# Band masks by edge, loads by half, and a new order of steps in a two-stage attention kernel

## The chip, the cores and the metric

The kernel runs on one core of a Trainium2 chip. A core has a matrix engine (PE, with its weight loads, PEld), a vector engine (DVE), a scalar engine (ACT), a general engine (POOL) and an engine that only issues transfers (SP). They run their own instruction streams, each in order, and wait for one another by semaphores. SP, ACT and POOL each issue DMA transfers into a queue of their own. The metric is the device time of one execution in microseconds. 181.07 us is the median of three runs of the kernel before.

## The reference

Two layers. The first is a local attention over 4 batches, 8 heads, 768 positions and a head size of 64. Each query sees the keys less than 16 positions away, and one summary for each of the 24 blocks of 32 positions: the maximum of the block's keys, and the mean of its values.

```python
k_sum = k.reshape(B, H, nb, block, D).max(axis=3)
v_sum = v.reshape(B, H, nb, block, D).mean(axis=3)
mask_l = np.abs(pos[:, None] - pos[None, :]) < window
scores_s = scale * np.einsum('bhsd,bhnd->bhsn', q, k_sum) + np.log(block)
scores_all = np.concatenate([np.where(mask_l, scores_l, -1e9), scores_s], axis=-1)
attn = softmax(scores_all) @ np.concatenate([v, v_sum], axis=2)
```

The second takes the result, with the heads joined (512 columns), through four causal attention experts of one head each; a gate picks two of the four per position and weighs their outputs.

```python
for e in range(E):
    q, k, v = x @ wq[e], x @ wk[e], x @ wv[e]
    ye = causal_softmax(scale * q @ k.T) @ v @ wo[e]
    out += (gate weight of e, 0 if not among the top two) * ye
```

## The kernel before

**Names of steps.** The kernel is a list of some 740 steps. Each step is a few instructions, with a kind, a batch b, and a pair of heads c (0 to 3) or a group g of two pairs; `sc010` is the first half of the scores of batch 0, pair 1. `TABLE` gives the order in which the steps are issued, the engine of each (V, A, G, S, P for DVE, ACT, POOL, SP, PE) and the buffers that it takes. Since each engine runs in order, the order of an engine's steps in the table is its queue. Step numbers in the table count the steps as they are declared. An entry `f` puts in matmuls on zeros; the first number is the bank, the second their count.

**First layer, for each pair of heads.** `dk`, `dq` load four heads of keys or queries, cast to half precision, from POOL; for batch 0, group 0 in two parts of two heads each (`parts`). Both parts write one buffer `kn` or `qn`, and whoever reads it waits for both. `dv` loads the values of a pair in 24 blocks of 64 positions, rows 0 to 63 of a block, beginning 16 positions before it (L277 to L281). `hc` copies rows 0 to 31 of each next block into rows 64 to 95, so that a block holds its whole band of 96 positions; it leaves out the last block of each head. `vq` copies the last rows of a head and zeroes rows 0 to 15 of each head's first block (L288). `vz` once zeroes the rows behind each head's end, and `vone` writes the column that sums the weights, zero where the value rows are zeroed. The block sums of the values come in two ways: `bs` (matmuls with a selection matrix, L306), `be` (their sum out of PSUM, DVE, L324) and `ds` (a copy into rows 96 to 119 of every block); or, for the groups in `TREE`, `dvs` (a second load of the values from SP, L341), `tr` (a tree of additions on POOL, L355) and `ds`. Then `tk` turns the keys (L373), `kw` lays them out by blocks, `rk` takes the maxima (L393), `ksc` appends them; `tq` and `cq` turn the queries. `sc` starts with a matmul that writes the band mask (L426) and adds the scores of six blocks (L432); `ex` is the exponential (L440), `av` the product with the values (L450), `rc` and `xm` the division, `tx` a transpose (L477), `hi` and `lo` a split into two half-precision numbers.

**Second layer, for each batch.** `pp` (projections, L640) and `pc`; `vp` (values and gate, L570), `lg`, `v2`; `ga` to `gc` the gate; `sp` (scores, L664), `es` (exponential, L672), `dm` (causal cut on POOL, L677), `aw` (L688), `r2`, `wv`, `tw`, `ct`, `op` (L750), `oc`, and `od` (the store).

The buffers are few: three of `kn` and `qn`, six of values, one tree buffer, eight PSUM banks. The copies are recorded under the lines of a helper: L164 on ACT, L166 on the others. The first layer of one batch is interleaved with the second layer of the one before.

Of the kernel before, what the change touches and what calls it, by code (L numbers as in the profile page):

```python
# [25 lines left out]
TREE = {(1, 1), (2, 0), (2, 1), (3, 0), (3, 1)}  # L26
# [26 lines left out]
4,V, 18,S,0 10,G, 8,V, 17,V, 0,V, f,P,0.8 7,V, 112,S, 20,A, 13,G,0 15,G, 14,G,0 16,G, 30,G,1 11,G, 1,G, 61,P,1  # L53
5,V, 62,A,0 63,V,0 44,P,0 64,V, 45,A,1 f,P,2.5 31,G,1 78,P,0 79,A,2 9,G, 2,G, 3,V, 46,V,0 65,P,2 48,P,3 99,P,0
204,G,0 49,V,0 82,P,1 66,A,1 24,S,1 19,V, 205,G,2 47,A, 32,S,2 21,P,3 80,V,0 22,V,0 6,G, 52,P,4 83,A,2 81,A,
50,P,1 53,A,0 95,P,6 100,A,0 246,P,7 51,A,1 96,V,1 97,V,0 26,V, 98,G, 229,P,3 67,P,4 68,A,2 25,G, 224,S,0 69,P,0
250,P,2 251,V,1 84,P,4 70,A,3 230,A,0 23,G, 216,G,0 86,P,0 33,G, 27,P,6 28,V,1 87,A,4 247,A,2 85,A,5 248,V,0
34,A, 55,P,0 231,V,1 54,P, 29,G, 56,V,0 103,P,4 104,A,1 35,P,6 71,P,4 57,V,0 36,V,1 38,S,3 39,G, 58,P,0 59,V,0
37,A, 120,G, 60,V,0 72,P, 73,V,0 74,V,0 89,P,6 88,P, 40,A, 101,P,0 102,A,5 41,P,4 280,P,5 90,V,0 91,V,1 42,V,1
43,V, 232,A, 281,A,1 249,G, 254,P,0 255,A,4 252,P,6 92,P,2 93,A,1 206,S,4 209,S,0 233,P,4 234,V,1 116,S,0 115,S,  # L60
117,S,1 225,G, 94,V,1 263,P,5 113,S, 105,P,0 211,A, 106,P, 253,A,5 107,V,0 108,V,1 235,P,2 236,A,1 114,A, 75,P,6
109,P,0 110,V,2 111,V,2 76,A,3 210,G, 208,G, 207,G, 77,V,3 221,S,2 212,P,2 213,V,1 122,G, 264,A,2 166,P,3
168,P,0 217,G,2 119,A, 167,A,0 226,G,0 218,S,3 12,G, 121,A, 169,V,1 227,G, 127,P,6 129,V,0 179,P,0 180,A,0
282,V,1 128,V,0 265,V,0 182,P,2 183,A, 130,P,4 132,A, 124,P,0 214,G, 125,A, 385,S,0 283,V, 131,V, 126,A, 176,P,2
170,P,6 171,A, 267,P,4 139,P,0 133,V,5.0 134,A, 177,A, 223,V, 268,V,0 140,V,2 228,G, 237,P,6 284,P,4 238,A,3
215,G, 266,G, 285,V,1 269,P,2 173,P,0 270,A,2 172,G, 240,P,6 135,V, 136,V,0 239,P, 174,A, 271,P,2 272,A,1 118,S,
123,A, 185,P,0 137,P,4 286,P,2 186,A, 287,A,3 241,V,0 242,V,1 243,P,6 288,P,0 138,V,0 150,P,4 222,V, 289,A,0
257,P,2 244,V,0 245,V,0 151,A,1 220,G, 144,P,0 378,G,2 256,P, 258,V,0 259,V,1 377,G,0 424,P,4 425,V,1 145,A,
386,G, 403,P,5 404,A,1 379,A,0 290,P,0 291,P, 156,P,4 157,A, 147,P,2 260,P,6 261,A,1 390,G,1 219,G, 181,G,
274,P,4 273,P, 148,A, 184,G, 292,V,0 293,V,0 262,V,1 153,P,0 154,A, 275,V,0 276,V,1 187,G, 565,G,1 294,P,2  # L70
295,A,2 632,P,6 296,V,2 387,G,0 392,S,1 437,P,7 277,P,4 278,A,3 149,G, 146,G, 155,G, 279,V,3 420,P,0 407,P,1
559,S,0 566,S,3 421,V,2 438,A,0 408,A,0 339,P,2 340,A,1 341,P,4 178,G, 388,G, 391,G,2 158,G, 175,G, 141,P,2
633,A,2 190,P,0 188,P, 342,A,0 189,P, 346,P,4 422,V,0 423,G, 352,P,6 564,G,0 389,V,2 405,V,0 380,G, 142,A,
191,V,0 192,V,0 406,V, 300,P,2 347,A,0 143,G, 303,P,4 382,A, 301,A,0 302,V,1 381,G, 152,G, 193,P,0 353,A, 305,A,
355,P,6 394,V, 304,A, 560,G, 349,P,2 356,A, 357,G, 297,P,4 350,A, 561,G,0 310,P,6 299,V, 159,P,2 298,A, 439,V,0
194,V,0 348,G, 384,G, 161,P, 160,P, 162,V,0 358,P,0 311,A,2 359,A, 411,P,6 412,A,2 343,P,4 344,A, 312,P,0
# [12 lines left out]
635,A,4 486,P,0 487,A,1 602,P,2 603,A,2 525,G, 337,P,4 338,V,0 611,P,7 612,V,2 534,G, 558,G, 636,P,0 637,A,3
520,P,4 481,A, 482,V, 521,A, 522,G, 519,G, 484,P,2 529,P,0 613,V,1 485,A,0 530,A, 615,P,7 616,V,2 483,V,0  # L90
587,P,4 588,P, 589,V,0 614,G, 600,P,2 601,A,0 575,G, 488,P,0 489,A,1 567,G, 490,G, 374,P,6 375,A,1 590,V,1
571,G, 531,G, 368,P,4 369,V,0 619,P,0 620,A,5 617,P,2 618,A,1 591,P,6 500,P,4 592,V,0 622,P,0 621,P, 593,V,0
370,A, 623,V,0 624,V,1 605,P,2 604,P, 606,V,0 503,P,6 501,A, 504,A, 607,V,0 625,P,0 626,A,1 627,V,1 494,P,4
639,P,6 528,G, 491,P,2 638,P, 495,A, 497,P,0 505,G, 492,A, 608,P,4 498,A, 640,V,0 371,P,2 641,V,1 642,P,0 502,G,
609,V,2 535,P,6 643,A,3 610,V,2 537,P, 644,V,3 536,P, 538,V,0 372,A,0 658,P,4 660,P,0 693,P,2 659,V,0 539,V,0
661,A,1 373,A, 493,G, 677,P,0 678,A,0 665,P,6 666,A, 694,V,2 674,P,4 651,P,0 668,P,6 671,P,2 675,A, 669,A,
670,G, 200,S, 691,P,4 672,A, 652,V,0 653,V,1 662,P,6 540,P,0 663,A, 692,A,0 648,P,2 649,V, 496,G, 650,V, 499,G,
507,P,6 541,V,0 506,P, 508,P, 509,V,0 510,V,0 376,S, 707,P,2 701,P,0 708,A,1 645,P,4 511,P,6 698,P,2 702,A,
647,V, 646,V, 673,G, 667,G, 699,A, 512,V,2 710,P,0 711,A, 695,P,4 676,G, 709,G, 696,A, 703,G, 545,P,6 664,G,
679,G, 654,V,2.0 655,A, 681,P,0 656,V, 682,P, 546,A,0 547,S, 704,P,3 705,A, 657,V,0 680,P, 683,V,0 684,V,0  # L100
687,V, 548,P,6 549,A,1 550,S, 542,P,2 688,V, 543,A,2 544,S, 700,G, 697,G, 706,G, 712,G, 715,P,4 714,P, 713,P,
720,V,0 689,P,2 690,A,0 685,P,0 721,V,1 722,P,6 686,A, 723,V,2 716,V, 717,V, 733,P,6 736,A,0 737,A, 718,P,4
730,P,7 719,V, 724,P,4 734,V,1 735,S, 731,V,2 732,S, 725,A,0 726,S, 727,P,0 728,A,1 729,A,
# [51 lines left out]
def make_plan(nc, T, q, k, v, moe_w_gate, moe_wq, moe_wk, moe_wv, moe_wo, out):  # L155
# [3 lines left out]
    def en(e):  # L159
        return getattr(nc, ENG[e])  # L160
# [17 lines left out]
    vones, vz, kwpad, v2one, knpad = st("vones"), st("vz"), st("kwpad"), st("v2one"), st("knpad")  # L178
# [7 lines left out]
    def masks(e):  # L186
        nc.gpsimd.memset(T["mt"], 0.0)
        for h0 in (0, 64):
            w = T["mt"][h0:h0 + 64, 0:WIN]
            nc.gpsimd.affine_select(w, w, [[-1, WIN]], AL.is_ge, NEG, base=31, channel_multiplier=1)  # L190
            nc.gpsimd.affine_select(w, w, [[1, WIN]], AL.is_ge, NEG, base=-1, channel_multiplier=-1)
# [8 lines left out]
    def vone(e):  # L200
        t = T["vball"]
        en(e).memset(t[0:96, :, 0:24, 64:65], 1.0 / XS)
        en(e).memset(t[96:128, :, 0:24, 64:65], 32.0 / XS)
        en(e).memset(t[0:16, :, 0:24:NQ, 64:65], 0.0)
        en(e).memset(t[64:96, :, NQ - 1:24:NQ, 64:65], 0.0)
        en(e).memset(t[64:80, :, NQ - 1:24:NQ, 64:65], 1.0 / XS)
# [8 lines left out]

    def vzero(e):
        t = T["vball"]
        en(e).memset(t[64:96, :, NQ - 1:24:NQ, 0:64], 0.0)
# [17 lines left out]
    def vtzero(e):  # L236
        for t in T["vt"]:
            en(e).memset(t, 0.0)

    qn, kn = {}, {}  # L240
# [694 lines left out]
```

## Time and profile before

| | |
|---|---|
| runs | 180.6, 181.07, 185.0 us |
| profiled execution | 177.54 us, its span 175.8 us |
| mean granted clock of PE | 0.956 |
| busy: PE, PEld | 148.6, 108.8 us |
| busy: DVE, ACT, POOL | 122.7, 124.9, 104.9 us |
| moved by DMA | 25.60 MB |
| chain that ended last | PE 42%, DMA 24%, ACT 10%, POOL 8%, DVE 7%, issue 6% |

A busy share is a mean over the whole span, and matmuls are pipelined, so PE's busy time is no measure of its peak. Where the time goes is read stage by stage, from the idle time of PE and what ended it. The chain names, for each moment, what the work that ended last was waiting for.

### The profile page before, as it was taken

To read this page: it belongs to the slowest core of one execution; us is meant where nothing else is said; L and a number is where in the kernel's file an instruction comes from. 1 tells how busy PE (TensorE), PEld (TensorE's weight loads), DVE (VectorE), ACT (ScalarE), POOL (GpSimd) and SP (SyncE) were. 2 spreads that over 40 slices of the span, in tenths; PEclk is the share of its full clock that TensorE was granted. 3 is DMA by queue.
4 is the path that set the end of the run, shared out by engine and by line. 5 is a ranking of instruction groups with operands and counts; after the bars stand their busy time and mean duration, and the time that the engine had idled before them with its cause. 6 is when DMAs were issued, how large, how long until landed. Compare 5 with 4: busy or idle time off the path is not lost.

```text
span 175.8 us, 6926 instructions
## 1 busy us (share of the span) xinstructions
PE 148.6 (85%) x3005; PEld 108.8 (62%) x3005; DVE 122.7 (70%) x244; ACT 124.9 (71%) x160; POOL 104.9 (60%) x181
## 2 busy tenths in 40 slices
PE   0667973999896999999998899869999999999760
PEld 0236752798764777867755488648765875675420
DVE  6345566579795987799985788872896986277630
ACT  2344686169948986899687977868989583969650
POOL 8962059746965798379959999927978200324100
PEclk9995699579999999999999999999999999999998
DMA  5999999999998699999969938991001502101846
GB/s 94 181 195 198 216 186 148 152 201 193 153 197 228 80 170 188 173 194 171 150 106 175 181 55 191 250 248 49 4 4 62 183 4 75 44 4 35 300 157 229
DMA packets 44894, 25.60 MB, mean 146 GB/s; under 512 B 33344, under 2 KB 39744, under 8 KB 44864
## 3 DMA queue, kind: packets, MB, share of 16 engines
q1 hardware_dynamic: 33200, 16.08, 47.7%
q0 software_dynamic: 6432, 6.29, 23.5%
q10 hardware_dynamic: 5232, 2.79, 7.7%
q8 instruction: 23, 0.38, 1.0%
q14 instruction: 7, 0.06, 0.1%
HBM read 25.16 MB, written 6.29 MB: 179 GB/s over the span
## 4 chain that ended last, share of the span: by engine, by line
PE 42%; DMA 24%; ACT 10%; POOL 8%; DVE 7%; issue 6%; POOLq 0%; ACTq 0%; DVEq 0%
DMA vb<-in_v_dram 11%; PE ps L450 9%; DMA kn<-in_k_dram 8%; PE ps L640 6%; DMA qn<-in_q_dram 5%; PE ps L570 4%; PE ps L688 4%; ACT a L672 3%; PE ps L664 3%; PE ps L750 3%; PE ps L477 3%; PE ps L373 3%; POOL vb L166 3%; PE ps L306 2%; PE ps L426 2%
## 5 line engine op out<-in xcount | busy, mean ns | idle before, releaser
L672 ACT ACTIVATE a<-ps 128x1024 f16<-128x1024 f32 (+1 forms) x48 | 42.5, 922 | 5.6 <-PE ps L664 4.0
L677 POOL TENSOR_SCALAR_AFFINE_SELECT a<-a 128x256 f16<-128x256 f16 x48 | 19.1, 421 | 28.4 <-ACT a L672 25.1
L440 ACT ACTIVATE aT<-ps 120x768 f32<-120x768 f32 x32 | 25.4, 815 | 9.1 <-PE ps L432 6.9
L450 PE MATMUL ps<-vb,aT 120*64 120x65 f32 x768 | 28.1, 231 | 3.3 <-issue 2.3
L450 PEld LDWEIGHTS ps<-vb,aT 120*64 120x64 f32 x768 | 25.6, 145 | 6.4 <-issue 4.0
L355 POOL TENSOR_TENSOR vt<-vt 120x1024 f32<-120x1024 f32 (+3 forms) x20 | 24.1, 1205 | 1.0
L640 PE MATMUL ps<-hi,wqk 128*128 128x384 f16 x128 | 22.6, 326 | 0.4 <-DVE lo L495 0.3
L166 POOL COPY vb<-vb 16x128 f32<-16x128 f32 (+1 forms) x20 | 14.1, 712 | 9.7 <-DMA vb<-in_v_dram 8.9
L164 ACT COPY kw<-ps 128x1152 f16<-128x1152 f16 x13 | 14.4, 1122 | 7.5 <-PE ps L373 7.5
L393 DVE TENSOR_REDUCE ks<-kw 128x24 f16<-128x768 f16 x16 | 14.9, 943 | 4.8 <-ACT kw L164 4.5
L640 PEld LDWEIGHTS <-wqk 128*128 128x128 f16 x128 | 11.9, 97 | 8.4 <-issue 1.2
L664 PE MATMUL ps<-qk,qk 64*128 64x512 f16 (+3 forms) x128 | 15.8, 307 | 1.0 <-DVE wT L166 0.7
L570 PE MATMUL ps<-wvg,hi 128*128 128x264 f16 x96 | 13.9, 275 | 3.0 <-ACT a L672 1.5
L465 DVE TENSOR_TENSOR x<-ps,rec 128x768 f32<-128x768 f32 x16 | 15.3, 958 | 1.0 <-PE ps L477 0.5
L495 DVE TENSOR_TENSOR lo<-ps,hi 128x768 f16<-128x768 f32 x16 | 15.0, 955 | 1.5 <-ACT hi L164 1.0
L166 POOL COPY vb<-vu 24x768 f32<-24x768 f32 x18 | 14.8, 823 | 1.0
L688 PE MATMUL ps<-v,a 128*128 128x65 f16 x336 | 12.3, 194 | 0.6 <-POOL a L677 0.6
L688 PEld LDWEIGHTS <-a 128*128 128x128 f16 x336 | 11.2, 97 | 2.3 <-issue 0.9
L750 PE MATMUL ps<-wo,wT 128*128 128x512 f16 x48 | 12.0, 380 | 0.5 <-DVE wT L166 0.5
L432 PEld LDWEIGHTS <-kw 64*128 64x128 f16 x384 | 10.4, 98 | 2.8 <-issue 0.7
L426 PE MATMUL ps<-pi,mt 64*128 64x384 f16 x64 | 11.4, 345 | 0.3 <-DVE qT L166 0.3
L432 PE MATMUL ps<-qT,kw 64*128 64x64 f16 x384 | 11.5, 195 | 0.0
(106 smaller groups left out, 269.7 us busy)
## 6 DMA issues: line engine op xcount, KB each, us to landing
vb<-in_v_dram SPq DMA_DIRECT2D x12, 400.0 KB
out_dram<-ob SPq DMA_DIRECT2D x8, 512.0 KB
vt<-in_v_dram SPq DMA_DIRECT2D x20, 192.0 KB
kn<-in_k_dram POOLq DMA_DIRECT2D x7, 384.0 KB, 7.6
qn<-in_q_dram POOLq DMA_DIRECT2D x7, 384.0 KB, 6.3
out_dram<-ob ACTq DMA_DIRECT2D x3, 512.0 KB
vb<-in_v_dram ACTq DMA_DIRECT2D x2, 400.0 KB
vb<-in_v_dram SPq DMA_DIRECT2D x2, 384.0 KB
```

The source lines that it names most:

```text
L166: en(e).tensor_copy(dst, src)
L355: en(e).tensor_tensor(y, p, q_, AL.add)
L432: nc.tensor.matmul(s[:, hp, 64 * t:64 * t + 64], T["kw"][kw.slot][r, tt, :], T["qT"][qT.slot][r].rearrange("c (s p) -> c s p", s=8)[:, :, ...
L440: nc.scalar.activation(T["aT"][aT.slot][0:KR], pbank(sc, 2)[0:KR, :, 0:384], AF.Exp, scale=SCALE)
L450: nc.tensor.matmul(pbank(av, 2)[o:o + 64, u, 65 * (2 * (t // 2) + hp):65 * (2 * (t // 2) + hp) + 65], a[0:KR, hp, 64 * t:64 * t + 64], T[" ...
L570: nc.tensor.matmul(p[:, i, 0:264], hi_(ch)[:, cols], T["wvg"][:, ch, :], start=(ch == 0), stop=False, skip_group_check=True)
L640: nc.tensor.matmul(pbank(pp, 2)[:, u, 0:384], T["wqk"][:, cc, ch, j, :], hi_(ch)[:, 384 * u:384 * u + 384], start=(ch == 0), stop=(ch == N ...
L664: nc.tensor.matmul(pbank(sp, 2)[:, ep, c0:c0 + w], T["qk"][qk[1].slot][r, 128 * tj:128 * tj + 128], T["qk"][qk[0].slot][r, n0:n0 + w], sta ...
L672: nc.scalar.activation(a2v(u), pbank(sp, 2)[:, :, 0:ln], AF.Exp, scale=SCALE / (XS * XS))
L677: nc.gpsimd.affine_select(m, m, [[0, 2], [1, 128]], AL.is_ge, 0.0, base=0, channel_multiplier=-1)
L688: nc.tensor.matmul(pbank(av, 2)[:, ep, 65 * ti:65 * ti + 65], a2v(u)[:, ep, o:o + 128], T["v2"][v2.slot][:, tj, 2 * cc + ep, :], start=(tj ...
L750: nc.tensor.matmul(pbank(op, i1 - i0)[:, ti - i0, :], T["wT"][wTs[cc].slot][:, 128 * ti:128 * ti + 128], T["wo"][:, cc, :], start=(cc == 0 ...
```

## The change

- **Masks.** Three band masks instead of one: for inner blocks, for the first block of a head (rows 0 to 15 masked), and for the last (columns 80 to 95 masked). Each `sc` step has two mask matmuls per head, of 64 and 320 columns, in place of one of 384. `vz` and all `vq` steps go. `hc` now copies all 24 blocks, and `vone` writes no zeros.
- **Loads.** Each half of `dk` and `dq` has its own signal (`kr`, `qr`), and `tk` and `tq` wait for theirs; all of batch 0 is loaded in halves.
- **Sums.** Group (1,1) leaves the tree, so `dvs11` and `tr11` go and `bs12`, `be12` come.
- **SP.** `hc` may be a load of its own from DRAM (hc12, hc30, hc33), and `ds` a transfer within SBUF (ds01, ds11, ds13, ds23, ds32, ds33), both from SP.
- **Order.** A new table. POOL: dk001, dk010, dq001, dq000, rid, dk000, id16, dk011, mt, dq010, dk100, dq011, sel, v2o, hc01, ksc00 and so on. ACT: dv02, dv01, kw01, cq01, hc02, dv00, ex010, and so on. SP: dv03, ds01, the weights, dv11, dv13, dv10, dvs20, dv12, hc12, dvs30, dwo, ds11, ds13, dv20, dv21 and so on. PE begins with tk01, tq01, tk02, tq00, sc010, sc011, tk00; its fills are five matmuls after that and two ahead of av010, in place of eight at the start and five after tk00. Of the `kw` copies 9 stay on ACT (13 before), of the `pc` copies 8 (11 before).

```diff
-TREE = {(1, 1), (2, 0), (2, 1), (3, 0), (3, 1)}
+MT3 = 3
+TREE = {(2, 0), (2, 1), (3, 0), (3, 1)}
...
-            w = T["mt"][h0:h0 + 64, 0:WIN]
...
+            w = T["mt"][h0:h0 + 64, :, 0:WIN]
...
+        nc.gpsimd.memset(T["mt"][:, 1, 0:16], NEG)
+        nc.gpsimd.memset(T["mt"][:, 2, 80:WIN], NEG)
...
-    def vzero(e):
-        t = T["vball"]
-        en(e).memset(t[64:96, :, NQ - 1:24:NQ, 0:64], 0.0)
...
+        for r in (kr, qr):
+            w = [st("part") for _ in range(parts)]
+            r[b, 2 * g], r[b, 2 * g + 1] = w[0], w[-1]
...
-        def ends(e):
-            w = T["vb"][vb[b, c].slot]
-            copy(e, w[64:80, NQ - 1:24:NQ, 0:64], w[0:16, NQ:25:NQ, 0:64])
-            en(e).memset(w[0:16, 0:24:NQ, 0:64], 0.0)
...
+            if e == "S":
+                nc.sync.dma_start(out=w[64:96, 0:n, 0:64], in_=rows(48, 32, 64, n))
...
+                copy(e, w[64:96, 0:24, 0:64], w[0:32, 1:25, 0:64])
...
+                if e == "S":
+                    for h in range(2):
+                        nc.sync.dma_start(
+                            out=T["vb"][vb[b, c].slot][WIN:KR, NQ * h:NQ * h + NQ, 0:64],
+                            in_=T["vs"][t.slot][WIN:KR, i, 64 * h:64 * h + 64].unsqueeze(
+                                1).to_broadcast((NSUM, NQ, 64)))
+                    return
...
-        R.step(f"tk{b}{c}", {"P": 0.38}, [kn[b, g], rid, knpad], [kp], tk, mode=2)
+        R.step(f"tk{b}{c}", {"P": 0.38}, [kr[b, c], rid, knpad], [kp], tk, mode=2,
+               keep=[kn[b, g]])
...
-                for hp in range(2):
-                    r = slice(64 * hp, 64 * hp + 64)
-                    nc.tensor.matmul(s[:, hp, 0:384], T["mt"][r, :], T["pi"][r],
-                                     start=True, stop=False, skip_group_check=True)
+                for m, t0, t1 in (((1, 0, 1), (0, 1, 6)), ((0, 0, 5), (2, 5, 6)))[u]:
+                    for hp in range(2):
+                        r = slice(64 * hp, 64 * hp + 64)
+                        nc.tensor.matmul(s[:, hp, 64 * t0:64 * t1], T["mt"][r, m, :],
+                                         T["pi"][r, t0:t1], start=(t0 == 0), stop=False,
+                                         skip_group_check=True)
...
-            load_qk(b, g, 2 if (b, g) == (0, 0) else 1)
+            load_qk(b, g, 2 if b == 0 else 1)
```

More of the change, by code (lines that the diff above doesn't have):

```diff
@@ L274, in dv @@
             dma = en(e).dma_start
+            if (b, c) == (B - 1, NCH - 1):
+                assert vb[b, c].slot in seen
+            seen.add(vb[b, c].slot)
             i0 = 1 if (b, c) == (0, 0) else 0
@@ L311, in sums @@
         R.step(f"bs{b}{cs[0]}", {"P": 0.03 + 0.054 * npair * 13 * 4 / 4},
-               [vs_[b, c] for c in cs] + [sel], [sp], mm, mode=3,
+               [vs_[b, c] for c in cs] + [vr[b, c] for c in cs] + [sel], [sp], mm, mode=3,
                keep=[vb[b, c] for c in cs])
@@ L361, in dsum @@
                     j = 32 * (2 * (c % 2) + h)
-                    copy(e, T["vb"][vb[b, c].slot][WIN:KR, NQ * h:NQ * h + NQ, 0:64],
-                         T["vu"][u.slot][j:j + NSUM, :].unsqueeze(1).to_broadcast((NSUM, NQ, 64)))
-            R.step(f"ds{b}{c}", {"G": 1.75, "V": 0.95, "A": 1.64}, [u], [vb[b, c]], dsum)
+                    dst = T["vb"][vb[b, c].slot][WIN:KR, NQ * h:NQ * h + NQ, 0:64]
+                    src = T["vu"][u.slot][j:j + NSUM, :].unsqueeze(1).to_broadcast((NSUM, NQ, 64))
+                    if e == "S":
+                        nc.sync.dma_start(out=dst, in_=src)
+                    else:
+                        copy(e, dst, src)
+            R.step(f"ds{b}{c}", {"G": 1.75, "V": 0.95, "A": 1.64, "S": 0.9}, [u], [vb[b, c]], dsum,
+                   dma=576 / 960)
     def stage1_pair(b, c, hs, ls):
@@ L408, in tq @@
                 turn(pbank16(qp), src, s, 96 * s, 96, T["id16"][0:96, 0:96])
-        R.step(f"tq{b}{c}", {"P": 0.34}, [qn[b, g], id16], [qp], tq, mode=2)
+        R.step(f"tq{b}{c}", {"P": 0.34}, [qr[b, c], id16], [qp], tq, mode=2, keep=[qn[b, g]])
         def cq(e):
@@ L804, in make_plan @@
     R.step("mt", {"G": 1.3}, [], [mt], masks)
-    R.step("vz", {"V": 2.6, "G": 3.0}, [], [vz], vzero)
     R.step("vone", {"V": 0.9, "G": 1.0}, [], [vones], vone)
@@ L867 @@
     one("rid", (128, 100), HALF)
-    one("mt", (128, 128), HALF)
+    one("mt", (128, MT3, 128), HALF)
     one("pi", (128, 6, 64), HALF)
```

136 lines of the change are left out of this document (69 added, 67 removed).

## The prediction

> **What bounds the kernel now.** I read the slices of the page first, then the engines by stage, the chain that ended last, the DMA queues stretch by stretch, and at the end the single durations.
>
> In the slices (40 of 4.4 us each) the eye goes to the holes of PE:
>
> ```profile
> PE   0667973999896999999998899869999999999760
> PEclk9995699579999999999999999999999999999998
> DMA  5999999999998699999969938991001502101846
> ```
>
> PE has holes in the first 31 us and at the very end, and is nearly full between. Its granted clock falls to 0.5 twice, at 13 to 22 us and at 31 to 40 us. The DMA engines are full from 4 us on. The same by stage (columns: length, then busy time of PE, PEld, DVE, ACT, POOL, then clock and DMA):
>
> ```profile
> 0.00:9.00 9.00, 3.27 (x8) 1.04 (x8) 4.56 (x12) 2.65 (x2) 7.89 (x21) 1.00 0.95 139
> 9.00:18.00 9.00, 6.47 (x122) 5.00 (x125) 4.54 (x9) 4.29 (x6) 3.65 (x11) 0.76 1.22 197
> 18.00:27.00 9.00, 7.13 (x196) 5.24 (x196) 5.65 (x11) 7.33 (x10) 2.99 (x5) 0.86 1.16 199
> 27.00:31.60 4.60, 2.21 (x50) 1.96 (x52) 2.45 (x5) 2.42 (x3) 4.02 (x11) 0.91 1.21 146
> 31.60:48.00 16.40, 15.61 (x406) 13.38 (x406) 12.65 (x23) 11.84 (x13) 10.82 (x18) 0.82 1.15 175
> 48.00:120.00 72.00, 65.78 (x1386) 49.24 (x1382) 58.19 (x107) 57.17 (x77) 55.25 (x81) 1.00 1.01 172
> 120.00:165.00 45.00, 44.57 (x828) 31.55 (x824) 31.44 (x72) 35.97 (x48) 20.29 (x39) 1.00 0.15 53
> 165.00:175.80 10.80, 3.54 (x26) 1.36 (x24) 3.24 (x10) 3.19 (x5) 0.00 (x0) 0.92 0.62 228
> ```
>
> So there are four stages. Up to 31.6 us PE waits for loads and for the work on the values; from 48 to 120 us it is idle for 6.22 us (72.00 less 65.78); from 120 to 165 us for 0.43 us; then a tail of 10.8 us. From 31.6 us on PE sets the time, so an edit pays if it lets the dense stage begin earlier, takes PE work out, or closes the 6.22 us. What starts the dense stage late, in the chain (start, length, what):
>
> ```profile
> 7.77 8.65 DMA qn<-in_q_dram
> ...
> 25.52 1.48 POOL vb L166
> 27.04 1.09 PE ps L450 x29
> 28.13 2.34 issue
> 30.47 1.13 PE ps L450 x19
> ```
>
> and in the timeline of POOL and PE (in brackets the idle time before, and its releaser):
>
> ```profile
> 23.83 1.02 POOL L166 COPY kw<-ks 128x288 f16<-128x288 f16 x1 [9.62 <-DVE ks L393]
> ...
> 32.28 1.51 PE L306 MATMUL ps<-vb,sel 80*32 80x128 f32 x24
> ...
> 40.77 0.34 PE L426 MATMUL ps<-pi,mt 64*128 64x384 f16 x2
> 40.95 0.34 PE L432 MATMUL ps<-qT,kw 64*128 64x64 f16 x12
> 41.12 0.33 PE L426 MATMUL ps<-pi,mt 64*128 64x384 f16 x2
> ...
> 45.68 0.96 PE L477 MATMUL ps<-id,x 64*128 64x64 f32 x24 [0.61 <-ACT aT L440]
> 46.57 1.53 PE L306 MATMUL ps<-vb,sel 80*32 80x128 f32 x48
> 48.04 2.77 PE L640 MATMUL ps<-hi,wqk 128*128 128x384 f16 x16
> ```
>
> The last query of the first group lands at 16.4 us, because its issue stood behind other POOL work. POOL then stands 9.62 us in front of one copy (ksc03), and vq01, ds00, vq02, ds01 queue behind it. The value matmuls (L450) therefore come at 27.0 and again at 30.5 us, with a hole of 2.34 us, after which PE runs at half clock. The first projection (L640) starts at 48.04 us; I use it as the mark where the two orders can be compared.
>
> **The change, part by part.**
>
> *First loads.* Two rows of the queues, from 9 to 15 us and from 3 to 4 us (packets, MB, share):
>
> ```profile
> q0 software_dynamic: 945, 0.92, 90.8%
> q1 hardware_dynamic: 997, 0.25, 31.2%
> ```
>
> ```profile
> q1 hardware_dynamic: 809, 0.21, 134.7%
> ```
>
> POOL's queue and SP's move the same number of packets, 158 and 166 per us, though a key packet is four times a value packet; a value queue by itself moves 809 per us. A value load (1600 packets of 256 B) takes 2 us alone and 10 us beside keys. The Trainium skill, "DMA: Bandwidth & Descriptors", Queues, rings and completion order, says that a DMA engine takes turns between queues by packets; the rows agree. Its Rules for kernel authors say that spreading DMAs over issuing engines brings no bandwidth; by that the second value queue is worth nothing (the late-values rival below), by the turns it doubles the values' share.
>
> ```profile
> kn<-in_k_dram POOLq DMA_DIRECT2D x2, 192.0 KB, 5.2
> ```
>
> The keys: POOL issues dk001 at about 0.85 instead of 1.70 us, since id32 no longer stands ahead. At 5.2 us to landing (the median of the two half loads of keys) that is 6.0 us; each further half (192 packets) is 1.2 us later: dq000 9.7, dk000 10.9, dq010 13.3 and, behind dk100, dq011 17.0 us. Each tk or tq now waits for its own half alone. Each was waiting on transfers of 384 packets before.
>
> The values: dv03 on SP and dv02 on ACT, dv01 behind dv02. About 1 us of 809 packets shared by both gives 400 each, the other 1200 at 166 per us take 7.2 us: both end near 11 us. Then dv01: 900 packets until the keys are through at 16.5 us, the last 700 at 809 per us: 17.4, landed at 18 us.
>
> *What then waits.* Behind hc01, which stands on POOL until dv01 lands, are ksc00, dk110, ds03 and dq100. The durations:
>
> ```profile
> L166 POOL COPY vb<-vb 32x1408 f32<-32x1408 f32 x8 | 10.8, 1352 | 2.2 <-DMA vb<-in_v_dram 1.8
> L166 POOL COPY kw<-ks 128x288 f16<-128x288 f16 x5 | 3.1, 619 | 10.9 <-DVE ks L393 10.7
> L324 DVE TENSOR_TENSOR vs<-ps,vs 24x128 f32<-24x128 f32 x14 | 4.1, 292 | 0.5
> L166 POOL COPY vb<-vb 16x128 f32<-16x128 f32 x12 | 3.4, 286 | 7.5 <-DMA vb<-in_v_dram 7.1
> L288 POOL MEMSET vb<- 16x128 f32 x12 | 2.3, 196 | 0.7
> L164 ACT COPY kw<-ps 128x1152 f16<-128x1152 f16 x13 | 14.4, 1122 | 7.5 <-PE ps L373 7.5
> L166 DVE COPY kw<-ps 128x1152 f16<-128x1152 f16 x3 | 4.1, 1352 | 0.5 <-PE ps L373 0.5
> ```
>
> ```profile
> 0.82 0.74 SPq L277 DMA_DIRECT2D vb<-in_v_dram  x1
> ```
>
> ```profile
> GB/s 0 0 0 0 0 0 0 0 0 82 228 257 270 219 175 164 168 170 167 148 132 146 160 182 183 202 223 245 223 206 187 202 174 144 163 176 204 194 198 191
> ```
>
> The second of these is the DMA rate from 0 to 10 us in forty slices: SP's first issue, at 0.82, moves its first bytes at 2.25 us.
>
> hc01 at 18.0 + 1.47 (1352 ns, by 1536/1408 columns) = 19.5; ksc00 + 0.62 = 20.1; on PE sc000, cold, twice its 0.35 (40.77 to 41.12) = 20.8; bs03 and bs01, cold, 1.5 each (the row of 32.28) = 23.8; be01 on DVE, four operations of 0.29 = 25.0. ds01 is now a DMA from SP, which no row shows for SBUF to SBUF: two issues of 0.74 and 1.4 us to the first packet (0.82 to 2.25), then 576 packets, 0.7 us at the free rate or 3.5 us beside keys; together 2.8 (the second issue lies beside the first transfer) to 6.4 us; I take 3.0, nearer the free row, since POOL's queue has run empty behind hc01. So av010 starts at 28.0 us.
>
> ```profile
> 135.65 2.95 PE ps L450 x96
> ```
>
> From there to the projection PE has eight value steps of 0.74 (96 records in 2.95 us), three score steps of 0.35, two key or query transposes of 0.42, four of 0.5 (two L477 steps take 0.96 at 45.68): 9.8 us at full clock. I add 2.4 us, of which 1.7 is a first stretch of 3.4 us at half clock: some 40.2 us, against 48.04. By 48.04 the old order had also done bs10 (1.46), two score steps (0.70) and tk13 and tq10 (0.84): 3.0 us. The gain is 7.8 - 3.0 = **4.8 us**. If dv01 lands with dv02, the DVE queue sets be01 some 3 us earlier: 7.8. If the keys never run dry, dv01 lands 3.5 us later, and if PE stays cold through it another 3 us go: a loss of 1.7.
>
> *PE's added work.* (1,1) leaves the tree, so bs12 adds one more step like that of 46.57: + 1.46 us (46.57 to 48.04). The three masks split one mask matmul in two, 64 more in all with 64 more weight loads. The columns streamed stay 384, and the score step of 0.35 already fits 14 loads: from 0 to 0.1 us per step (two L426 loads in the timeline), 32 steps, 0 to 3.2 us; I take 0.03, the pace of a score pair (12 matmuls in 0.17): **+ 1.0**. The opening fill of eight is gone; PE has nothing waiting behind it then, so I cost it at 0 here and put the clock into the bounds.
>
> *Relief and load of the other engines.*
>
> ```profile
> L355 POOL TENSOR_TENSOR vt<-vt 120x1024 f32<-120x1024 f32 (+3 forms) x20 | 24.1, 1205 | 1.0
> ```
>
> POOL loses 12 vq (0.286 + 0.196): 5.8 us; one of five trees, 24.1 / 5 = 4.8 and its last short add; and five value copies net of about 1.5. DVE loses vz and four vq. Between 48 and 120 us DVE takes kw, pc and oc steps from ACT (1352 against 1122 ns for kw) and gives v2 and lg steps back; summed step by step that is 5.5 us more on DVE and some 8 less on ACT. SP gets nine waits for finished sums in its queue: the loads of the third batch (dv20, dv21) stand behind ds11 and ds13, those of the fourth behind ds23 and ds33. They already waited there for the tree's buffer. Of the 6.22 us of holes, POOL, ACT and late loads made the larger part; I take **- 2.5**. Ends: - 5 (POOL and ACT no longer bind) and + 5.5 (DVE binds throughout).
>
> *Tail.* Same steps, two on other engines: 0, within 1.
>
> Sum: - 4.8 + 1.46 + 1.0 - 2.5 = **- 4.8 us**, a span of 171.0. The profiled execution took 177.54, 1.74 over its span: 172.7. The median of the runs shown, 181.07, is 1.0199 times that execution: **176.1 us**. Runs of this kernel spread from 180.6 to 185.0, so 2% is about what a measurement can tell from no change.
>
> **The rivals.**
>
> 1. *Late values.* The second queue brings nothing or the first loads stay behind the keys: dv01 lands at 22 us, and the prologue's gain shrinks to 0.5 or so. Then - 0.5 + 2.46 - 2.5 = - 0.5: 180.5 us. For it: 166 packets per us beside keys. Against: POOL stops issuing keys while it waits for dv01, which frees the engines. The Trainium skill, "TensorE: Matmul & The Clock Gate", Part 4: PE-mode transpose, adds that transposes don't lift the clock; without the opening fill that would keep PE cold longer. The row at 9 to 18 us, with transposes and fills at 0.76, can't separate the two. It is the same case, up to 3 us further. Chance 0.24.
> 2. *DVE becomes the bound* (slower). Place: 75 to 90 us, where DVE is already the fullest engine. Price: its 5.5 us of added work becomes PE idle time, in place of - 2.5: - 4.8 + 2.46 + 5.5 = + 3.2, 184.3 us; beyond 2% if a further 0.4 us of the prologue's gain is lost. It decides from about 2.3 us of added PE idle time on. For it, the row below: 14.50 of 15. Against: before and after that DVE is at 72 to 81%. Chance 0.21.
>
> ```profile
> 75.00:90.00 15.00, 14.16 (x228) 10.24 (x223) 14.50 (x21) 12.22 (x19) 13.15 (x19) 1.00 1.25 165
> ```
>
> 3. *More than forecast*: the holes close and dv01 lands early: - 7.8 + 2.0 - 4 = - 9.8, 170.9 us. Chance 0.12.
>
> **How the numbers follow.** Forecast 0.43, late values 0.24, DVE 0.21, more 0.12. Faster by over 2% (below 177.4) holds the forecast and the third: 0.55. Within 2%: 0.24. Slower, of which nearly all by over 2% if it comes, as DVE and cold PE add up: 0.21. The range is 169.5 (just under the third rival; the lower ends of all terms together give 169.5 too) to 184.5, just over the second; all upper ends together (+ 12) would be worse, at less than 1 in 10.
>
> **What will show it.** dk001's transposes should start by 6.5 us, the first scores near 11 us, hc01 on POOL near 18 us with an idle time of about 6 us ahead of it, av010 near 28 us, the first L640 near 40 us, and the stage after it should hold less than 4 us of PE idle time until the loads end. PE should lose no more than 3 us to added work. Wrong if L640 starts after 45 us, if ds or hc transfers on SP take over 5 us to land, or if PE's idle time between 45 and 120 us grows.

## The result and the profile after

The changed kernel takes 192.52 us (median of four runs, 190.94 to 194.42), the kernel before 181.95 beside it. The ratio is 1.0795, with a 95% interval of 1.0662 to 1.0929: slower by 8%, where 176.1 us and a gain were forecast. The profiled execution took 192.66 us, its span is 190.9, and PE's granted clock 0.924 (before: 177.54, 175.8 and 0.956). Ratios here compare, for each kernel, the runs within 1.5% of its fastest one, and medians are of all runs; by medians the change costs 5.8%. The kernel before ran again beside each experiment, with medians from 179.72 to 180.93 us; against these the loss is some 12 us.

First a correction. The change's list of ACT's steps above, and the prediction after it, read the new table wrongly. ACT's queue is dv02, **kw01, dv01**, cq01, hc02, dv00, ex010: the second load of values stands behind a copy that waits for the first keys.

The slices of the changed kernel, 40 of 4.8 us:

```profile
PE   0077499399989969689989887989999999996860
PEclk9999855559999985999999999999999999999998
DMA  5999972967999956998989777984958000231446
```

PE begins two slices in, where the kernel before had its fill, the clock is at half for four slices, and DMA, full in every slice from 4 to 53 us before, has holes at 30 and 42 us. By stage (length, busy time of PE, PEld, DVE, ACT, POOL, then clock, DMA share and GB/s):

```profile
0.00:9.00 9.00, 0.00 (x0) 0.00 (x0) 3.19 (x5) 1.28 (x1) 7.32 (x21) 1.00 0.94 132
9.00:18.00 9.00, 6.82 (x145) 5.30 (x147) 6.42 (x9) 3.39 (x3) 3.14 (x12) 1.00 1.24 204
18.00:27.00 9.00, 5.37 (x104) 4.00 (x99) 3.99 (x8) 3.01 (x4) 2.64 (x4) 0.72 1.09 146
27.00:31.60 4.60, 4.60 (x104) 3.77 (x100) 3.34 (x7) 3.38 (x4) 3.59 (x7) 0.50 0.30 51
31.60:48.00 16.40, 13.12 (x302) 11.09 (x296) 10.29 (x20) 7.52 (x9) 5.04 (x10) 0.67 0.85 133
48.00:120.00 72.00, 62.65 (x1338) 47.33 (x1332) 49.45 (x94) 51.64 (x70) 42.41 (x53) 0.95 0.98 153
120.00:165.00 45.00, 44.33 (x896) 33.15 (x893) 32.67 (x56) 33.65 (x47) 20.40 (x34) 1.00 0.50 96
165.00:190.90 25.90, 16.99 (x260) 10.76 (x258) 13.45 (x39) 13.78 (x18) 4.54 (x12) 0.97 0.45 164
```

PE's idle time between 48 and 120 us is 9.35 us (72.00 less 62.65), where it was 6.22. Over the whole span it is 37.0 us against 27.2, and the other 5 us of the longer span are busy time of PE (153.9 us against 148.6), much of it at half clock. DVE was busy for 49.45 us between 48 and 120, 8.7 less than before; the steps of the new order come later, so part of that is work that falls behind 120 us.

Where it starts, in the timelines of PE, ACT, POOL and SP:

```profile
9.39 0.87 PE L390 MATMUL ps<-rid,kn 98*64 98x98 f16 x16 [9.39 <-POOL mt L195]
...
36.92 4.17 PE L470 MATMUL ps<-vb,aT 120*64 120x65 f32 x72 [3.26 <-DMA vb<-vs]
...
50.20 2.76 PE L660 MATMUL ps<-hi,wqk 128*128 128x384 f16 x16 [0.37 <-DVE lo L515]
```

```profile
10.30 0.61 ACTq L281 DMA_DIRECT2D vb<-in_v_dram  x1
...
14.98 5.28 ACTq L283 DMA_DIRECT2D vb<-in_v_dram  x1
20.31 0.81 ACT L460 ACTIVATE aT<-ps 120x768 f32<-120x768 f32 x1 [5.57 <-issue]
```

```profile
21.65 1.46 POOL L166 COPY vb<-vb 32x1536 f32<-32x1536 f32 x1 [9.25 <-DMA vb<-in_v_dram]
```

```profile
SPq L337 <- DVE vs L328: 28.4, 1, 28.4
```

The first keys are turned at 9.39 us, not 6.5: dk001, issued at 1.37, takes 7.9 us to land, and the POOL work that the profile names ends only by chance at the same time. dv01 is issued at 10.30, the moment at which kw01 can begin. The next value load, dv00, holds ACT itself: its second, small issue (L283) lasts 5.28 us, and ex010 behind it begins only at 20.31. hc01 begins on POOL at 21.65 us. And SP, after its one value load, stands 28.4 us in front of ds01, whose sum comes from DVE; the weights, dv11, dv13, dv10 and dvs20 are behind it. av010 (the first L470 row) begins at 36.92 us and the first projection (L660) at 50.20, where the kernel before had it at 48.04. For two stretches nothing is left to move (same columns as above, 28.5 to 31.5 and 41.2 to 44.2 us):

```profile
28.50:31.50 3.00, 3.00 (x70) 2.41 (x66) 1.90 (x6) 2.46 (x3) 2.22 (x7) 0.50 0.03 6
41.20:44.20 3.00, 3.00 (x84) 2.48 (x78) 2.75 (x5) 1.51 (x2) 2.08 (x7) 0.79 0.02 6
```

DMA moved 6 GB/s there. The chain that ended last (start, length, what) shows what that costs 40 us later:

```profile
30.00 0.96 SPq L337
...
33.51 2.40 SPq L537
...
36.60 5.08 DMA a<-in_moe_wq_dram
41.81 1.17 POOL wqk L166 x2
...
43.44 5.39 DMA vb<-in_v_dram
48.98 1.47 POOL vb L166
...
51.18 1.84 POOL vt L235
...
55.63 9.69 DMA vt<-in_v_dram
65.48 2.38 POOL vt L367
...
68.52 1.29 POOL vt L367
...
74.14 5.45 DMA vt<-in_v_dram
79.72 2.35 POOL vt L367
```

Most links are queues in order: ds01 holds the weights, these hold POOL's casts; the values of batch 1 (dv11, issued at 43.44) hold hc11 on POOL, that holds vtz (L235), and vtz holds dvs20, the token sums of batch 2. One link the chain names wrongly, that from the casts to dv11. SP's list of waits has another releaser for it:

```profile
SPq L281 <- PE ps L470: 5.6, 1, 5.6
```

dv11 takes the buffer of dv01, and the value matmuls of pair 1 (L470) read that buffer until 43.34 us. So dv11 is held by the late start itself, whatever queue it stands in: in runs 1, 2, 3, 6 and 9 below, too, it is issued within 0.1 us of the end of these matmuls. In the kernel before, where vtz ran at 5.10 us, all trees together waited 1.0 us (the L355 row above).

### The profile page after: what moved, and what is told of

It is laid out like the page before. It is cut to its first block, busy times and chain, and to the rows that moved or that the text cites. A ratio compares the mean times of both kernels' runs of the same rounds, so it can differ in the third digit from the quotient of the medians.

```text
span 190.9 us, 7107 instructions
## 1 busy us (share of the span) xinstructions
PE 153.9 (81%) x3111; PEld 115.4 (60%) x3111; DVE 122.8 (64%) x235; ACT 117.6 (62%) x152; POOL 89.1 (47%) x151
## 4 chain that ended last, share of the span: by engine, by line
PE 41%; DMA 17%; POOL 16%; DVE 9%; issue 7%; SPq 6%; ACT 1%; DVEq 0%; POOLq 0%
DMA vt<-in_v_dram 8%; PE ps L470 7%; PE ps L660 6%; PE ps L770 5%; POOL vt L367 5%; PE ps L708 5%; PE ps L590 4%; PE ps L684 3%; DMA kn<-in_k_dram 3%; PE ps L390 3%; DMA vb<-in_v_dram 3%; DMA a<-in_moe_wq_dram 3%; SPq L353 3%; POOL vb L166 2%; PE ps L497 2%
## 5 line engine op out<-in xcount | busy, mean ns | idle before, releaser
L470 PE MATMUL ps<-vb,aT 120*64 120x65 f32 x768 | 28.9, 233 | 7.3 <-DMA vb<-vs 5.5
L697 POOL TENSOR_SCALAR_AFFINE_SELECT a<-a 128x256 f16<-128x256 f16 x48 | 18.3, 406 | 35.0 <-ACT a L692 34.5
L470 PEld LDWEIGHTS ps<-vb,aT 120*64 120x64 f32 x768 | 26.1, 146 | 12.1 <-issue 7.0
L367 POOL TENSOR_TENSOR vt<-vt 120x1024 f32<-120x1024 f32 (+3 forms) x16 | 19.6, 1225 | 14.5 <-DMA vt<-in_v_dram 13.6
L660 PE MATMUL ps<-hi,wqk 128*128 128x384 f16 x128 | 23.2, 329 | 0.4 <-DVE lo L515 0.4
L166 POOL COPY vb<-vb 32x1536 f32<-32x1536 f32 x8 | 11.7, 1460 | 20.3 <-DMA vb<-in_v_dram 20.1
L390 PE MATMUL ps<-rid,kn 98*64 98x98 f16 (+1 forms) x256 | 9.8, 228 | 10.3 <-POOL mt L195 9.4
L660 PEld LDWEIGHTS <-wqk 128*128 128x128 f16 x128 | 11.8, 98 | 8.7 <-issue 1.7
L164 ACT COPY kw<-ps 128x1152 f16<-128x1152 f16 x9 | 10.0, 1119 | 9.8 <-PE ps L390 9.7
L310 PE MATMUL ps<-vb,sel 80*32 80x128 f32 x192 | 10.3, 382 | 6.1 <-issue 3.6
L684 PE MATMUL ps<-qk,qk 64*128 64x512 f16 (+3 forms) x128 | 14.7, 306 | 0.4 <-DVE kw L166 0.3
L390 PEld LDWEIGHTS <-kn 98*64 98x64 f16 (+1 forms) x256 | 7.8, 125 | 11.8 <-issue 10.5
L452 PE MATMUL ps<-qT,kw 64*128 64x64 f16 x384 | 13.3, 209 | 0.6 <-issue 0.6
L445 PE MATMUL ps<-pi,mt 64*128 64x320 f16 (+1 forms) x128 | 13.1, 284 | 0.7 <-issue 0.7
```

The lines of the kernel that those rows point to most:

```text
L166: en(e).tensor_copy(dst, src)
L367: en(e).tensor_tensor(y, p, q_, AL.add)
L390: nc.tensor.matmul(dst[64 * hp:64 * hp + 64, c0:c0 + eye.shape[-1]], src[0:n, hh + hp, 64 * s:64 * s + 64], eye, is_transpose=True)
L470: nc.tensor.matmul(pbank(av, 2)[o:o + 64, u, 65 * (2 * (t // 2) + hp):65 * (2 * (t // 2) + hp) + 65], a[0:KR, hp, 64 * t:64 * t + 64], T[" ...
L660: nc.tensor.matmul(pbank(pp, 2)[:, u, 0:384], T["wqk"][:, cc, ch, j, :], hi_(ch)[:, 384 * u:384 * u + 384], start=(ch == 0), stop=(ch == N ...
L684: nc.tensor.matmul(pbank(sp, 2)[:, ep, c0:c0 + w], T["qk"][qk[1].slot][r, 128 * tj:128 * tj + 128], T["qk"][qk[0].slot][r, n0:n0 + w], sta ...
```

## The experiments

The two theories at the start: the loss is made by transfers that stand in in-order queues (theory A: dv01 behind kw01 on ACT, the weights and later loads behind ds01 on SP), or by what comes after the start (theory B: the split masks, DVE's added steps, the new order). Table entries in the diffs are step number, engine, buffer, with the name behind.

**1. Values on SP.**

```diff
 36,S,0   dv03
+22,S,2   dv01
+17,S,3   dv00
...
-22,A,2   dv01
-17,A,3   dv00
```

> The changed kernel with dv01 and dv00 issued from SP, right behind dv03, in place of ACT; nothing else moved. Theory A (the loss comes from transfers that stand in an engine's own queue): hc01 on POOL begins near 17 us in place of 21.65, ex010 on ACT near 14.7 in place of 20.31, av010 near 33 in place of 36.92, and the time falls by about 4 us, to 188. Theory B (the loss comes from the steady state: DVE's added steps, the split masks on PE, the new order): the prologue moves as said, but the end stays within 1 us of 192.

Measured: 190.57 us, ratio 1.059 [1.0497, 1.0682], by the ratios 2% below the changed kernel (the intervals just overlap).

```profile
19.68 1.46 POOL L157 COPY vb<-vb 32x1536 f32<-32x1536 f32 x1 [7.08 <-DMA vb<-in_v_dram]
```

hc01 is 2 us earlier, and everything behind ds01 about 3 us; av010 begins at 33.97 us and ex010, with dv00 no longer ahead of it on ACT, at 15.53, both near what theory A had. The time lies between the two theories: a small part of the loss.

**2. ds01 on POOL.**

```diff
-26,S,   ds01
+26,G,   ds01
```

> The changed kernel with ds01 as a copy on POOL at its place in the table, so that SP waits for nothing ahead of the weights and the values of the second batch. Theory A: av010 near 33.5 us in place of 36.92 (be01 ends at 30.0, the copy takes 1.47, a wait behind other POOL work), the weights' casts no longer wait for their loads at 41.8, the tree loads of batch 2 are issued before 53 us, and the time falls by 5 to 9 us, to 184 to 187. If the weights and later values, now early on SP's queue, take the first keys' share instead, av010 stays after 36 us. Theory B: 191 to 193.

Measured: 193.5 us, ratio 1.0737 [1.0597, 1.0877]: no gain. With SP free the weights are issued at 1.64 to 19.34 us, beside the first keys and values, and hc01 moves to 24.05 us. The queue had also kept the weights out of the way. dv11, with nothing to wait for on SP since 19.34 us, is issued only at 40.48, when its buffer comes free.

**3. Both.** The edits of 1 and 2.

> Both edits: dv01 and dv00 on SP behind dv03, ds01 on POOL. Theory A: av010 near 30 us, the first L660 near 43, the time 178 to 182, that is the kernel before within 2%. Theory B: 188 or more.

Measured: 188.63 us, ratio 1.0418 [1.0306, 1.0529]. A third of the loss goes by medians (3.9 of 12 us), half by the ratios. The start is now as theory A had it, with av010 at 31.41 us and the first projection at 43.82; the time is as theory B had it. So most of what is left lies behind the start. One part of it is seen on POOL (the changed kernel has the same wait, 9.66 us):

```profile
58.70 2.36 POOL L358 TENSOR_TENSOR vt<-vt 120x1024 f32<-120x1024 f32 x1 [9.47 <-DMA vt<-in_v_dram]
```

The tree of batch 2 still waits 9.47 us for dvs20, issued at 46.45 us behind dv11, dv13 and dv10 and behind vtz.

**4. The masks alone, on the kernel before.** Three masks, hc over all blocks, no vz, no vq but the last block's.

```diff
-    def vzero(e):
...
-                    nc.tensor.matmul(s[:, hp, 0:384], T["mt"][r, :], T["pi"][r],
+                for m, t0, t1 in (((1, 0, 1), (0, 1, 6)), ((0, 0, 5), (2, 5, 6)))[u]:
```

> The kernel before with the three masks alone: 128 mask matmuls in place of 64, hc over all blocks, no vz, no vq but one (the very last block, whose last rows no load fills), vone without its zeros; order, engines and loads as before. The step times of sc tell the price: by my term of 0.03 us a step the time rises by 1.0 us less what 6 us of POOL work was worth, so 181 to 183; by the upper bound of 0.1 us a step 184; by theory B's reading that the masks are part of the loss, 184 or more; by theory A 180 to 182.

Measured: 184.34 us; one run of 180.64, the other three 184.18 to 187.49. These are too far apart to decide; run 13 repeats it.

**5. No copies on SP.** As 3, and the other eight copies that the change gave to SP on POOL.

```diff
-210,S,   ds11
+210,G,   ds11
```

(and so ds13, ds23, ds32, ds33, hc12, hc30, hc33.)

> The changed kernel with the third experiment's edits (dv01 and dv00 on SP behind dv03, ds01 as a POOL copy) and the other eight copies that it gives to SP as transfers (ds11, ds13, ds23, ds32, ds33, hc12, hc30, hc33) on POOL as well, each at its place in the table. The whole computation is done. Theory 1 (what is lost after 48 us is lost to transfers that stand in SP's queue and that queue up there for sums not yet made): the queue is then free of waits for other engines, the second half of the loss goes as well, 178 to 183 us. Theory 2 (the loss is in when the token sums of batch 2 start: dvs20 behind vtz and behind dv11, dv13, dv10): 185 to 189, since dvs20 keeps its place. Theory 3 (the order of the steps as a whole): 186 or more.

Measured: 201.48 us, four runs from 195.8 to 202.21, the slowest of all. The theory that SP's transfers as such make the loss falls. In POOL's queue hc12 now stands between vtz and the first tree. It needs dv12, which SP issues behind dvs20, at 49.82 us; POOL stands 10.91 us in front of it, and the tree begins at 61.35 us, where run 3 had 58.70.

**6. The tree's loads earlier.** As 3, and

```diff
+10,G,    vtz, ahead of hc01
 23,G,    hc01
...
 112,S,   dw10
+375,S,0  dvs20, behind dw10 and ahead of dv11
```

> The changed kernel with the third experiment's edits, vtz earlier on POOL (ahead of hc01) and dvs20 earlier on SP (ahead of dv11), the eight other SP transfers left as they are. The whole computation is done. Theory 1: 185 to 189, since the transfers of copies still stand in SP's queue. Theory 2: the 9.66 us that tr200 waits on POOL in the changed kernel goes, PE is 2 us busier between 60 and 90 us, 180 to 184. Theory 3: 186 or more.

Measured: 185.06 us, ratio 1.0196 [1.0056, 1.0337]. POOL and the stage (columns as above):

```profile
49.44 2.36 POOL L358 TENSOR_TENSOR vt<-vt 120x1024 f32<-120x1024 f32 x1
```

```profile
48.00:120.00 72.00, 65.98 (x1533) 50.57 (x1531) 54.24 (x98) 57.33 (x76) 46.42 (x63) 0.98 0.93 154
```

The tree begins at 49.44 us without waiting, and PE's idle time from 48 to 120 us is 6.02 us, as in the kernel before (6.22). SP's transfers of copies (ds11, ds13, ds23, hc12) are still there. The ratio's interval lies wholly below the changed kernel's; it overlaps that of run 3 a little.

**7. Edits of 5 and 6 together.**

> The edits of the two runs before together. Theory 1: 178 to 183, as without the earlier tree. Theory 2: 180 to 184. If the two causes add: 175 to 179, below the kernel before. Theory 3: 186 or more.

Measured: 187.99 us, ratio 1.0437 [1.0312, 1.0562]. In this order POOL seems the worse place for the eight copies, by 2.4% against run 6 (the intervals just overlap): POOL stands 5.77 us in front of hc12, and the tree begins at 56.22 us. Run 5, which differs from this one by vtz and dvs20 alone, is 13.5 us slower by medians: there hc12 and the tree behind it wait for a load that stands behind vtz and dvs20.

**8. SP transfers in the kernel before.** Run 4 with eight copies as transfers.

```diff
-215,G,   ds11
+215,S,   ds11
```

> The kernel before with the three masks (as in the fourth experiment) and eight copies as SP transfers: ds11, ds13, ds23, ds32, ds33, hc12, hc30, hc33, each at its place in the table of before. The whole computation is done. Theory 1: each of these transfers lands 3 to 5 us after its issue where the copy took 1 to 1.8 us, and SP stands still for their sums: 185 to 191. Theories 2 and 3: within 2 us of the fourth experiment, 179 to 183.

Measured: 188.83 us, ratio 1.0496 [1.0365, 1.0628]. Two waits, from the groups and from the list of waits:

```profile
L464 PE MATMUL ps<-vb,aT 120*64 120x65 f32 x768 | 29.3, 236 | 7.1 <-DMA vb<-vu 4.1 <-issue 2.0 <-POOL vb L158 0.9
```

```profile
POOL a L691 <- DMA vb<-vu: 7.6, 1, 7.6
```

So the same transfers cost nearly 3% in one order (1.0496 against 1.0207 in run 13) and seem to save 2.4% in the other: their price depends on the queue that they join.

**9. The tree's loads alone.** Run 6's edit on the changed kernel, nothing else.

> The changed kernel with one edit alone: vtz earlier on POOL (ahead of hc01) and dvs20 earlier on SP (ahead of dv11); the values' queues and ds01 stay as the change has them. The whole computation is done. If the two causes found so far add (the prologue's transfers, some 5 us, and the late token sums of batch 2, some 4 us): 187 to 190. If the tree's loads only pay once the values come early, because SP's queue stands behind ds01 until 30 us and dvs20 with it: 190 to 194. If the tree alone makes all of the loss after 48 us and the prologue's transfers none: 182 to 185.

Measured: 189.3 us, four runs of 183.5, 187.56, 191.04 and 192.51. By medians the tree's loads give 3.2 us, run 3 gives 3.9 and both 7.5, as two causes that add. The lowest run lies much nearer to the third theory, and the profile, which is of the highest, speaks for the second: its first tree begins at 54.64 us without a wait, 10.8 us earlier than in the changed kernel, yet its span is the same (190.8 us). These runs don't settle the split between the two.

**10. Two value queues alone, on the kernel before.**

```diff
-24,S,1   dv01
+24,A,1   dv01, ahead of hc00
```

> The kernel before with one edit: dv01 is issued on ACT, ahead of everything else there, so that the first values come on two queues; dv00, dv02 and dv03 stay on SP. The whole computation is done. By equal shares of packets per queue (158 of POOL's and 166 of SP's in the kernel before) POOL's keys get a third in place of a half while both value queues run: the last of the first keys and queries land 2 to 3 us later, dv01 not earlier than hc01 is reached in DVE's order (23.7 us): 180 to 184. If the values' arrival was what held the kernel before: 176 to 178. If neither: within 1% of the kernel before.

Measured: ratio 1.0014 [0.9947, 1.0082], median 182.47. The DMA list of its first 12 us (KB each, median to landing):

```profile
kn<-in_k_dram POOLq DMA_DIRECT2D x2, 192.0 KB, 7.7
```

The half loads of keys land in 7.7 us, where they took 5.2 with one value queue (8.2 in the changed kernel). The time does not change. hc01, on DVE behind the keys' work, begins at 25.17 us (23.69 before), so the second value queue buys nothing there. The Trainium skill, "DMA: Bandwidth & Descriptors", Rules for kernel authors, says that spreading DMAs over issuing engines brings no bandwidth. The trace agrees: in these 12 us the queues moved 1.77 MB, before 1.84. The loss of 2.5 us to another queue's load is the part to plan with.

**11. ksc03 behind ds00.** Run 4 with POOL's long wait moved.

```diff
-98,G,   ksc03
 23,G,   ds00
+98,G,   ksc03
```

> The kernel before with the three masks and one move: ksc03, for which POOL stood 9.62 us with ds00 and ds01 queued behind it, comes behind ds00. The whole computation is done. If that wait set the start of the value matmuls: 1 to 3 us below the fourth experiment's undisturbed 180.64, 177.5 to 179.5. If bs01, which waits for hc01 on DVE until 24.6 us and stands ahead of av001 on PE, set it: within 1 us of the fourth experiment, 179.5 to 181.5.

Measured: 183.58 us, ratio 1.0154 [1.0092, 1.0215], no faster than run 13. POOL's wait of 9.62 us (9.45 in run 13) was not what set the value matmuls: they begin at 27.05 us with the move and at 27.04 without it. Nor did it make the hole of 2.34 us that the prediction read beside it. That hole lies inside a step, after 29 of 48 matmuls, and run 13, with the wait as it was, has none there; what it is stands in the last section. A longest wait need not be on the path.

**12 to 14. The split mask matmul.** Some 2% were open. Run 12 adds the split to the kernel before, run 13 repeats run 4 with more rounds, run 14 takes the split out of run 6 and uses the inner mask everywhere, so it leaves out the masking at the ends of a head.

```diff
-                    nc.tensor.matmul(s[:, hp, 0:384], T["mt"][r, :], T["pi"][r],
-                                     start=True, stop=False, skip_group_check=True)
+                for t0, t1 in (((0, 1), (1, 6)), ((0, 5), (5, 6)))[u]:
...
+                        nc.tensor.matmul(s[:, hp, 64 * t0:64 * t1], T["mt"][r, :],
+                                         T["pi"][r, t0:t1], start=(t0 == 0), stop=False,
```

> The kernel before with one edit: each mask matmul of 384 columns is split as the change splits it, into 64 and 320, with the one mask it has; 64 more matmuls and 64 more weight loads on PE, nothing else. The whole computation is done. If the split costs PE time as the prediction had it (0.03 us a step) or more: 1 to 3 us slower, ratio 1.006 to 1.017. If PE hides it, as the spacing of the score steps in the changed kernel says (0.17 + 0.17 us as before): ratio within 0.995 to 1.005.

> The kernel of the fourth experiment again, which had one undisturbed run, now with more rounds. If the masks as a whole are what is left: ratio 1.012 to 1.02, as with ksc03 moved. If they cost nothing and ksc03's place did: 0.995 to 1.008.

> The changed kernel with the values' queues, ds01 and the tree's loads as in the sixth experiment, and the mask matmul in one piece with the first mask, so that the first and last token blocks of a head are not masked at the sequence's ends: that part of the computation is left out. If the split is what is left: 179 to 181.5, ratio at most 1.008. If not: as the sixth experiment, 182.5 to 184, ratio 1.015 to 1.025.

Measured: run 12 183.64 us, ratio 1.0186 [1.0016, 1.0356]; run 13 182.81, 1.0207 [1.0123, 1.029]; run 14 180.11, 0.9989 [0.9865, 1.0112]. All three point to the split as what was left, and without it the mended kernel is level with the kernel before. None is far from the noise. Run 12's interval starts just above 1, those of runs 6 and 14 overlap, and by medians (180.93 for the kernel before) runs 12 and 13 lose 1.5 and 1.0%. The loss is not in the mask matmuls' own time. By group (busy, mean ns), of the kernel before and then of run 13:

```profile
L426 PE MATMUL ps<-pi,mt 64*128 64x384 f16 x64 | 11.4, 345 | 0.3 <-DVE qT L166 0.3
```

```profile
L420 PE MATMUL ps<-pi,mt 64*128 64x320 f16 (+1 forms) x128 | 11.5, 258 | 4.1 <-ACT a L667 3.8 <-ACT aT L435 0.2
```

128 matmuls are busy for as long as 64. Runs 6 and 14 also differ in the time that PE stood with no releaser to be seen (total us, times, longest; run 6, then run 14):

```profile
PE ps L461 <- issue: 4.1, 2, 3.0
PE ps L443 <- issue: 2.3, 2, 1.8
```

```profile
PE ps L486 <- issue: 1.7, 1, 1.7
PE ps L441 <- issue: 1.0, 1, 1.0
PE ps L381 <- issue: 0.9, 1, 0.9
```

Run 6 loses 7.3 us to such stops in all (with two smaller ones), run 14 4.1 (with one). Run 13 loses 2.9, the kernel before 2.3, so in that order the stops explain little; and runs 4 and 13, the same kernel, have 4.6 and 2.9, so that the difference between runs 6 and 14 is no more than executions of one kernel show. What does go with the split is PE's clock. The mean granted clock of all runs is 0.931 and 0.934 in runs 12 and 13, 0.944 in the kernel before beside them; it is 0.952 in run 6 and 0.968 in run 14. In run 12's profile PE is busy for 152.8 us (before 148.6). Whether the split brings the lower clock or something else brings both was not shown, so how 64 more matmuls cost some 2 to 3.5 us is open.

## Why the prediction was wrong

The forecast failed first in the prologue, and then in what a late prologue does to the loads behind it. By the prediction's own reckoning, with the first projection at 50.20 us in place of 40.2 and 3.0 us of PE's work left for later, the gain of 4.8 us is a loss of 5.2: 10 of the 19.9 us by which the span was missed.

- **The keys** (forecast 6.0 us, turned at 9.39). The 5.2 us to landing came from a kernel with one value queue; with two it is 8.2 here and 7.7 in run 10. The prediction had the equal shares of the queues and used them for the values only. The issue also came at 1.37 us, not 0.85.
- **dv01** (forecast 18.0, hc01 began at 21.65). This was a misread queue: dv01 "behind dv02" was behind kw01. The condition of the first rival, dv01 at 22 us, came true almost to the digit, but by luck: the rival thought of the queues' shares, and dv01 was late because it was issued at 10.30 us. Its price of 180.5 us did not come true, since the rest of its sum was that of the forecast.
- **ds01** (forecast 3.0 us, from issue to use 6.9: 30.00 to 36.92). The low end was taken, because POOL's queue was to have run empty; the upper one of 6.4 was near. dq100 was issued at 30.38 us, right beside ds01, and from 32 to 35 us POOL's queue moved 334 packets and SP's 356. av010 began at 36.92, not 28.0.
- **The loads behind it.** "They already waited there for the tree's buffer" is the step that failed for the holes. It looked at the loads of batches 3 and 4 and passed over those right behind ds01: the weights, dv11, dv13, dv10 and dvs20. It also gave no price to vtz, which the new table puts behind hc11 on POOL. SP stood for 28.4 us, but run 2 took that wait away and gained nothing by itself, since the weights then came beside the first keys. What carried the delay on was the buffer of dv01: late value matmuls, then dv11, hc11, vtz and dvs20, and the tree of batch 2 waited 9.66 us. Of the holes between 48 and 120 us the forecast took 2.5 us off; 3.1 were added. Runs 3 and 6 give some 7.5 of the 12 us to the start (the values' queue and ds01) and to vtz and dvs20.
- **Masks** (forecast + 1.0, bounds 0 to 3.2). Runs 12 and 13 give 1.9 and 2.1% by the ratios, some 3.5 us, and 2.7 and 1.9 us by medians; run 14 against run 6 gives 5.0 us by medians of separate rounds. The mechanism, 0.03 us more per score step, is not there: the mask matmuls are as busy as before. The size, if it is the split's, lay near the upper end or above it; the reason is not known.
- **bs12** (forecast 1.46). It takes 1.52 us in run 6, at 63.48 us and without a wait: the term was right there. In the changed kernel it takes 2.91 us at half clock, after a wait of 1.71 for its values, which the forecast did not have.
- **DVE as the bound** did not come: between 48 and 120 us PE waited for DVE for 1.4 us, before for 1.5. The slower side was right to have a chance, on the wrong mechanism.
- **The tail** (forecast 0, within 1): from 165 us on PE is idle for 8.9 us, before for 7.3. No run tested it.

## What to carry to other kernels

A step that waits and is moved to another queue must be priced by everything that it holds, and not by its own length: what stands behind it in the queue, and also what waits for the buffers that it keeps from coming free (dv11 here). The same eight transfers cost nearly 3% in one order and seem to have saved 2.4% in the other. A load on another queue takes its packets from the load that is needed first, so the landing time of the first one has to be worked out again with every queue that is added. And read an engine's queue from the table entry by entry before anything is built on it.

## What was not expected of the hardware

A DMA issue can hold its engine: dv00's second issue on ACT, of 12 KB, lasted 5.28 us, and ACT did no other work for 5.57 us before the exponential behind it. In run 1, with that load on SP, the exponential began 4.8 us earlier.

PE stops in the middle of a step, at the same places in several kernels. PE's order of steps is the same in the changed kernel and in run 6; the stops in the two (first the changed kernel):

```profile
109.58 0.29 PE L452 MATMUL ps<-qT,kw 64*128 64x64 f16 x8 [0.59 <-issue]
...
115.67 0.45 PE L470 MATMUL ps<-vb,aT 120*64 120x65 f32 x8 [1.80 <-issue]
...
126.39 0.31 PE L445 MATMUL ps<-pi,mt 64*128 64x320 f16 x2 [0.67 <-issue]
```

```profile
99.80 0.29 PE L443 MATMUL ps<-qT,kw 64*128 64x64 f16 x8 [0.48 <-issue]
105.19 0.45 PE L461 MATMUL ps<-vb,aT 120*64 120x65 f32 x8 [1.09 <-issue]
...
116.19 0.31 PE L436 MATMUL ps<-pi,mt 64*128 64x320 f16 x2 [0.39 <-issue]
```

The same three steps, with the same eight, eight and two matmuls left in them, 10 us apart in time. The last two of them return in all eight kernels with this order of PE (the changed one and runs 1, 2, 3, 5, 6, 7 and 9), 0.48 to 4.36 us long in front of the eight value matmuls and 0.39 to 3.13 in front of the two mask matmuls. Such stops are bound to a place in the instruction stream, then; their length is not, and other places show a stop in some of these kernels only. The DMA queues of run 6 show a queue of instructions (packets, MB):

```profile
q8 instruction: 24, 0.39, 1.1%
```

24 packets of 16 KB each. The stops go with them. The 16 profiles show 60 stops of this kind, and 57 of them end 2.3 to 3.3 us after a packet of this queue starts, whether the stop is 0.25 or 4.36 us long (the hole of 2.34 us in the kernel before: packet at 27.4 us, end at 30.47). An estimate from 24 packets in 181 us is that one moment in seven would have a packet so placed by chance. The other three stops stand in front of whole steps. So PE very likely waits there for its next instructions. The rate of these stops was not varied by itself, and, as said, they don't account for the price of the split.
